# A gated mix of full and windowed attention on one core: a scheduler's constants laid out stretch by stretch, x turned in bf16, and scaled V in one GpSimd operation

## The chip, the cores and the metric

One core of a Trainium2 chip. Times are device microseconds of one execution; the profile's span runs from the first to the last instruction and is about 2 us shorter. Most executions of a kernel agree within 0.3%. A ratio below is the mean time of one kernel's fast runs over that of the other's of the same rounds, so it is not quite the ratio of the medians that stand beside it.

## The reference, cut to what matters

```python
# S = 2048 tokens, D = 640, H = 32 heads of Dh = 20
def A(x, wqkv, wo):                       # full attention
    q, k, v = heads(x @ wqkv)
    p = softmax(q @ k.T * Dh ** -0.5)     # 2048 x 2048 for each of 32 heads
    return merge(p @ v) @ wo
def B(x, wqkv, wo):                       # 8 keys at distances 0, 2, ..., 14 back
    ...
g = sigmoid((x * gate_w).sum(-1))
return g * A(x, ...) + (1 - g) * B(x, ...)
```

The cost is in A's 32 x 2048 x 2048 exponentials: 2048 blocks of 128 keys x 512 queries, one head each.

## The kernel before

It is one Python program that plays a *model* of the engines while it records instructions: every task gets a start and an end in the model, and the next task is chosen by what the model says is free. The order in which the tasks come out is the program, and each engine runs its own list in that order. So a small change of any duration or constant can change the whole order.

A score tile holds two or three blocks. TensorE makes it (`qk`), ScalarE turns it into exponentials (`exp`), and two iterations later TensorE multiplies by V (`pv`). There are two score buffers, so the score matmul of tile s waits for the exponentials of tile s-2. A block can also "ride": it goes into the spare third bank, and the vector engine (DVE) makes its exponential as an integer approximation (`uD`) with three shifted copies (`eD`), each multiplied by V scaled by a constant (`vS`). The more blocks ride, the less ScalarE has to do.

```python
def exp(s):                                            # ScalarE
    T("act", actc(512 * n), lambda e: e.activation(
        ebuf[s % NE][:, 0:512 * n], score[s % 2][:, 0:512 * n], ACTF.Exp, scale=LN2 / STEP), ...)

def gen_d(d):                                          # a quad of up to 4 riding blocks
    ...
    for k in range(1, K):                              # K = 4
        T("pool", 0.7, lambda e, k=k: e.tensor_scalar(
            vS[:, d % 2, k - 1, :], vA_of(kb, q), WEIGHTS[k], None, op0=ALU.mult), ...)   # GpSimd, 84 columns
    for k in range(1, K):
        ...
        T("dve", 0.11 + 0.1334 * n, lambda e, k=k, sl=sl: e.tensor_scalar(
            eD[:, sl % NS, 0:512 * n], uD[d % 2][:, 0:512 * n], SHIFTS[k], None, op0=ALU.add), ...)

def filler(limit):                                     # matmuls on nothing, to keep TensorE active
    if sch.load(2.3) >= FILL:
        return False
    ...

def spend(limit):                                      # side work until the next score matmul is due
    while True:
        run_side(limit)
        ...
        if now + 0.32 > limit or ... or not filler(limit):
            clock[0] = now + 0.2

SLACK = (0.3, 0.68)                                    # how long after exp(s-1) side work may go on
XTOL = 0.17; DTIME = 12.0; BOOST = 4.1; ...            # some 18 constants, the same for the whole run
...
while pvg < NG:
    us = next_tile(); qk(s); exp(s)
    if ...: pv_slot(s)
    spend(exps[s - 1].end + SLACK[len(us) - 2]); s += 1
# the start, once: x in, transposed on TensorE into f32 PSUM, copied to SBUF
turn(0, 0, 3, 0); turn(0, 3, 5, 1)                     # 3 chunks in one score buffer, 2 in the other
x_out: ScalarE copies 3 x 512 columns, DVE 2 x 512
```

## Time and profile before

| | before |
|---|---|
| time, median (lowest to highest) | 863.25 us (862.87 to 863.6) |
| span of the profile | 860.4 us |
| exponentials on ScalarE | 732 for 1736 blocks |
| first exponential starts, last ends | 20.70 us, 848.48 us |
| need at the shortest spacing | 777.6 us |
| loss | 43.5 us |
| tail | 11.9 us |

*Need* and *loss* are worked out from the trace's records. The shortest start-to-start spacing of two exponentials is 904 ns for two blocks and 1331 ns for three, so 427 ns a block and 50 ns an instruction; the need is the sum of that. The loss is what the spacings of all exponentials add up to, less the need, less other ScalarE work between them (6.5 us). Start + need + other + loss + tail is the span.

The page before: busy time by engine, the chain of waits by engine, and three groups (line, engine, operation, tiles, count, then busy us and mean ns of one, then idle time before them).

```profile
span 860.4 us, 30961 instructions
...
PE 837.2 (97%) x13299; PEld 310.4 (36%) x13302; DVE 692.4 (80%) x1178; ACT 820.2 (95%) x766; POOL 220.4 (26%) x333
...
PE 77%; ACT 15%; DVE 4%; issue 3%; POOL 1%; DMA 1%; DVEq 0%; ACTq 0%
...
L1432 ACT ACTIVATE ebuf<-score 128x1024 bf16<-128x1024 f32 (+1 forms) x732 | 804.5, 1197 | 19.9 <-PE score L1409 16.0
...
L720 POOL TENSOR_SCALAR vS<-vA 128x84 bf16<-128x84 bf16 x234 | 140.7, 604 | 230.7 <-PE obank L1477 186.4
L728 DVE TENSOR_SCALAR eD<-uD 128x2048 int16<-128x2048 int16 x234 | 160.2, 709 | 10.3 <-PE obank L1477 9.9
```

ScalarE is 95% busy and TensorE 97%. But the 837 us of TensorE contain 408 quads (four matmuls side by side) of filler, 88 us at 216 ns each, the commonest start-to-start spacing of quads in this trace, and the exponentials' 804.5 us contain waiting: they need 777.6. Of the 43.5 us of loss only 16 us appear as ScalarE waiting for a score matmul.

The waits before (who waited for whom: us, times, longest), three lines:

```profile
ACT ebuf L1432 <- PE score L1409: 16.0, 41, 1.0
...
PEld obank L1477 <- POOL vS L720: 8.8, 33, 0.9
...
PEld obank L1477 <- DVE uD L1422: 1.6, 6, 0.5
```

And the start in two views of the same trace, the timeline of ScalarE and the groups of DVE:

```profile
20.70 1.02 ACT L1432 ACTIVATE ebuf<-score 128x1024 bf16<-128x1024 f32 x1 [0.79 <-PE score L1409]
```

```profile
L1141 DVE CAST xT<-score 128x1024 bf16<-128x1024 f32 x4 | 4.9, 1225 | 3.9 <-PE score L1125 3.9
```

### The profile page before, as it was taken

The numbers are of one execution on the slowest core, as the hardware profiler recorded it, in microseconds if no ns is written. First come the engines' busy times: TensorE is split into PE (matmuls) and PEld (weight loads), VectorE is DVE, ScalarE is ACT, GpSimd is POOL, SyncE is SP. The second block draws the span as 40 slices with busy tenths as digits, with TensorE's granted clock in tenths as the row PEclk, the third lists the DMA queues.
The fourth block names the chain that finished last, engine by engine and source line by source line (L and its number), as shares of the span: only waits on it lengthen the run. The fifth ranks groups of instructions, "written<-read, shape, count | busy, mean of one in ns | idle before, by whom it ended". The sixth has DMA issues, their size and how long they took to land.

```text
span 860.4 us, 30961 instructions
## 1 busy us (share of the span) xinstructions
PE 837.2 (97%) x13299; PEld 310.4 (36%) x13302; DVE 692.4 (80%) x1178; ACT 820.2 (95%) x766; POOL 220.4 (26%) x333
## 2 busy tenths in 40 slices
PE   8999999999999999999999999999999999999997
PEld 4333333343333433333333333333333333333323
DVE  6567787898888889887988879789798878989763
ACT  5999999999999999999999999999999999999994
POOL 5032042721322222221111223222142223123310
PEclk9999999999999999999999999999999999999999
DMA  9112231001010100011010000110010001100000
GB/s 300 33 30 54 45 73 32 16 13 30 25 28 20 38 11 21 5 44 39 18 33 17 6 19 21 32 47 8 20 28 20 6 17 33 46 6 21 14 6 32
DMA packets 40892, 28.16 MB, mean 33 GB/s; under 512 B 23733, under 2 KB 39557, under 8 KB 40757
## 3 DMA queue, kind: packets, MB, share of 16 engines
q1 hardware_dynamic: 40756, 26.20, 11.7%
q8 instruction: 105, 1.72, 0.8%
q14 instruction: 31, 0.25, 0.1%
HBM read 11.94 MB, written 2.62 MB: 17 GB/s over the span
## 4 chain that ended last, share of the span: by engine, by line
PE 77%; ACT 15%; DVE 4%; issue 3%; POOL 1%; DMA 1%; DVEq 0%; ACTq 0%
PE score L1409 23%; PE side L489 19%; PE obank L1477 18%; ACT ebuf L1432 14%; PE score L489 6%; PE obank L1498 4%; PE score L1498 3%; PE side L1498 1%; PE score L615 1%; PE side L814 1%; DMA oTd<-in_A_x_dram 1%; DVE uD L1422 0%; DVE oTt L689 0%; PE score L1125 0%; ACT xT L1139 0%
## 5 line engine op out<-in xcount | busy, mean ns | idle before, releaser
L1432 ACT ACTIVATE ebuf<-score 128x1024 bf16<-128x1024 f32 (+1 forms) x732 | 804.5, 1197 | 19.9 <-PE score L1409 16.0
L1409 PE MATMUL score<-qT,kT 32*128 32x512 bf16 x2048 | 292.1, 384 | 8.7 <-ACT ebuf L1432 6.3
L1422 DVE TENSOR_SCALAR uD<-score 128x512 int16<-128x512 f32 x312 | 208.5, 684 | 41.8 <-PE score L1409 39.3
L720 POOL TENSOR_SCALAR vS<-vA 128x84 bf16<-128x84 bf16 x234 | 140.7, 604 | 230.7 <-PE obank L1477 186.4
L728 DVE TENSOR_SCALAR eD<-uD 128x2048 int16<-128x2048 int16 x234 | 160.2, 709 | 10.3 <-PE obank L1477 9.9
L1409 PEld LDWEIGHTS score<-qT,kT 32*128 32x128 bf16 x2048 | 72.1, 91 | 260.9 <-issue 131.5
L1477 PE MATMUL obank<-ebuf,vA 128*21 128x512 bf16 x1736 | 160.8, 384 | 2.2 <-DVE oTt L689 0.8
L489 PE MATMUL side<-xT,kvw 128*32 128x256 bf16 (+2 forms) x2530 | 102.5, 279 | 0.9 <-DVE dst L593 0.6
L695 POOL TENSOR_TENSOR rcp<-rcp,gA 128x16 f32<-128x16 f32 x31 | 12.3, 397 | 345.3 <-DVE rcp L693 320.8
L1477 PE MATMUL obank<-eD,vS 128*21 128x512 bf16 x936 | 81.0, 379 | 0.0
L489 PEld LDWEIGHTS side<-xT,kvw 128*32 128x32 bf16 (+1 forms) x2530 | 60.5, 96 | 35.0 <-issue 19.8
L1477 PEld LDWEIGHTS obank<-ebuf,vA 128*21 128x21 bf16 x1736 | 39.0, 89 | 81.3 <-issue 63.6
L1498 PE MATMUL obank<-xT,zero 128*32 128x512 bf16 x664 | 56.0, 383 | 0.0
L1498 PE MATMUL score<-xT,ident 128*32 128x512 bf16 x628 | 53.0, 381 | 0.1
L800 DVE TENSOR_TENSOR stage<-qkvB 128x1280 bf16<-128x1280 bf16 x64 | 53.0, 855 | 0.1
L877 DVE TENSOR_TENSOR stage<-qkvB,repB 128x1280 bf16<-128x1280 bf16 x64 | 52.1, 838 | 0.0
L489 PE MATMUL side<-stage,ident 128*32 128x512 bf16 (+1 forms) x768 | 48.7, 346 | 0.0
L784 DVE CAST qkvB<-side 128x512 bf16<-128x512 f32 (+1 forms) x72 | 41.7, 589 | 6.7 <-PE side L489 6.1
L700 POOL TENSOR_TENSOR oN<-oTt,rcp 128x512 bf16<-128x512 f32 x31 | 34.8, 1122 | 2.4
L689 DVE STREAM_TRANSPOSE oTt<-obank 128x512 f32<-128x512 f32 x32 | 22.8, 712 | 14.5 <-PE obank L1477 14.3
L1477 PE MATMUL obank<-uD,vA 128*21 128x512 bf16 x312 | 30.3, 379 | 0.0
L1477 PEld LDWEIGHTS obank<-eD,vS 128*21 128x21 bf16 x936 | 23.4, 92 | 17.5 <-issue 2.5
(167 smaller groups left out, 639.0 us busy)
## 6 DMA issues: line engine op xcount, KB each, us to landing
repB<-eB SPq DMA_DIRECT2D x128, 32.0 KB
WqP<-in_A_wqkv_dram SPq DMA_DIRECT2D x16, 160.0 KB
stage<-in_B_wqkv_dram SPq DMA_DIRECT2D x1, 2400.0 KB
oTd<-oN SPq DMA_DIRECT2D x108, 20.0 KB
qT<-dst SPq DMA_DIRECT2D x104, 20.0 KB
out_dram<-outsb SPq DMA_DIRECT2D x12, 160.0 KB
kvw<-in_A_wqkv_dram SPq DMA_DIRECT2D x2, 800.0 KB
oTd<-in_A_x_dram SPq DMA_DIRECT2D x2, 640.0 KB
```

The source lines that it names most:

```text
L489: ins = e.matmul(o[j:k, :], l[:, j:k], r, start=(first and i == 0), stop=(last and i == n - 1), skip_group_check=True)
L700: T(en, c2, lambda e: e.tensor_tensor(oo, ii, ib, ALU.mult), reads=["rcp", "oTt"], writes=["oN0"])
L720: T("pool", 0.7, lambda e, k=k: e.tensor_scalar(vS[:, d % 2, k - 1, :], _ap(vA, (kb * NQ + q) * 4 * DV, [[1, 4 * DV]]), WEIGHTS[k], None, ...
L728: T("dve", 0.11 + 0.1334 * n, lambda e, k=k, sl=sl: e.tensor_scalar(eD[:, sl % NS, 0:512 * n].bitcast(I16), uD[d % 2][:, 0:512 * n].bitcas ...
L784: t = TB(dvc(n * TOK), lambda e, o=o, i=i: e.tensor_copy(o, i), reads=[("side", b)], writes=[key])
L800: TB(dvc(CN * TOK, 2), lambda e, w=w, ks=ks: e.tensor_tensor(prodB(w), qB[:, :, :], ks, ALU.mult), reads=["qB", "kB"], writes=[("prod", w) ...
L877: TB(dvc(CN * TOK, 2), lambda e, w=w, vs=vs, rr=rr: e.tensor_tensor(prodB(w), vs, rr, ALU.mult), reads=["vB", ("repB", w4 % 2)], writes=[( ...
L1409: ins = e.matmul(o, kT[32 * j:32 * j + 32, q, kb * P:(kb + 1) * P], qT[g % NQT][32 * j:32 * j + 32, :], start=True, stop=True)
L1422: t = T("dve", 0.69, lambda e: e.tensor_scalar(uD[d % 2][:, 512 * i:512 * (i + 1)].bitcast(I16), side[x], UOFF, 0.0, op0=ALU.add, op1=ALU. ...
L1432: exps[s] = T("act", actc(512 * n), lambda e: e.activation(ebuf[s % NE][:, 0:512 * n], score[s % 2][:, 0:512 * n], ACTF.Exp, scale=LN2 / S ...
L1477: ins = e.matmul(obank[32 * j:32 * j + DV, :], v, src, start=(kb == 0), stop=(last and k >= len(lst) - 4), skip_group_check=True)
L1498: ins = e.matmul(o[32 * j:32 * j + 32, :], w[:, 32 * j:32 * j + 32] if best else w[:, :], xT[:, 0, 0:512], start=bool(best), stop=bool(bes ...
```

## The change

The intent: a look-ahead search on the model picks the 18 constants anew for each stretch of ten or more tiles (57 entries); the start is shortened; and GpSimd makes the three scaled V of a quad at once.

```diff
+PLAN = {
+    0: ((0.3, 0.7), 0.26, 2.5, 1.0, 1.0, -1.0, 0.0, 12.0, 7.0, 9.64, 0.4, 0.5, 4.5, 4.21, 0.0, 0.85, 2, 0.0),
+    20: ((0.3, 0.7), 0.12, 2.5, 6.6, 1.0, -1.0, 0.0, 12.0, 7.0, 9.0, 0.5, 0.5, 4.5, 4.0, 0.0, 0.85, 2, 0.0),
 ... 54 entries cut; from tile 320 on most have SLACK (0.23, 0.48) and later FILL 0.77 to 0.8
+    730: ((0.23, 0.48), 0.39, 2.5, 6.6, 0.69, -0.91, 0.1, 9.78, 7.0, 10.56, 0.47, 0.49, 6.24, 1.5, 0.2, 0.89, 1, -3),
+}
@@ main loop
+        plan = PLAN.get(s) if acting else None
+        if plan:
+            (SLACK, XTOL, XPRIO, XLATE, DWAIT, DIDLE, DIDLE2, DTIME, DLOW, DLATE, DVE_AHEAD, DAHEAD, BOOST, XBOOST, RFILL,
+             FILL, HOLD, BOFF) = plan
@@ loads
     x_load(0, 4.2)
-    T("sp", 5.5, ... wk0 ...)
     x_load(1, 5.5)
-    T("sp", 6.0, ... wq0 ...)
-    x_load(2, 7.0)
-    x_load(3, 8.5)
+    T("sp", 6.0, ... wk0 ...)
+    x_load(2, 6.9)
+    x_load(3, 8.2)
+    T("sp", 9.0, ... wq0 ...)
@@ gen_d
-        for k in range(1, K):
-            T("pool", 0.7, lambda e, k=k: e.tensor_scalar(vS[:, d % 2, k - 1, :], ..., WEIGHTS[k], None, op0=ALU.mult), ...)
+        T("pool", 1.0, lambda e: e.tensor_tensor(
+            vS[:, d % 2, :, :], _ap(vA, ..., [[0, K - 1], [1, 4 * DV]]), _ap(vw, 0, [[1, K - 1], [0, 4 * DV]]), ALU.mult), ...)
@@ start: all five chunks of an x tile in one score buffer, as bf16
+                    ins = e.matmul(scb[s_][:, c * 512 + blk * P:...], _ap(xt, ...), ident[:, :],
+                                   start=True, stop=True, is_transpose=True, skip_group_check=True)
-        T("act", actc(1536), ...xT[:, 0:3, cols]...)
-        T("dve", dvc(1024), ...xT[:, 3:5, cols]...)
+        T("act", actc(1024), ...xT[:, 0:2, cols]...)
+        T("dve", dvc(1536, 2), ...xT[:, 2:5, cols]...)
 ... the first Q is projected after the last K, one block of V instead of two is made before the first scores, x_out(3) moves ahead of k_out(1) on ScalarE; a dozen default constants change
```

## The prediction

> **What bounds the kernel now.** ScalarE's stream of exponentials, interlocked with TensorE. The page gives ACT 820.2 us busy of 860.4 (95%), of which the exponentials are 804.5 us in 732 instructions. The chain of waits is PE 77%, ACT 15%, DVE 4%: they hand the score banks back and forth. In the timeline, the shortest start-to-start spacings of exponentials are 904 ns (1024 columns) and 1331 ns (1536): 427 ns per 512 columns plus 50 ns. So 1736 units in 732 instructions need 777.6 us. First start 20.7 us, last end 848.5. The difference, 827.8 - 777.6 - about 7 (other ACT work) leaves roughly 43 us lost, only 16 us of it shown as ACT waiting for PE; the rest hides in "busy" instructions. Tail after the last exponential: 11.9 us. DVE (80%) and GpSimd (26%) are not limits.
>
> **What changes** (instruction orders of both):
>
> 1. Exponentials: 1720 units in 738 instructions, because DVE takes 328 score blocks instead of 312 (82 quads for 78). ACT need: 1720 x 0.427 + 738 x 0.050 = 771.1 us, -6.5 us, all critical. DVE pays 16 x 0.68 + 12 x 0.71 = +19 us, off the path.
> 2. Schedule. TensorE fillers fall from 408 quads to 306 (87 to 65 us at 0.213 us). Summing PE work between successive score matmuls, with durations read from the trace, against the exponential it must fit under: the local excess falls from 100 to 73 us. The measured loss was about 0.43 of that sum, so I estimate -12 us of loss (between -4 and -18). This main term is the most doubtful: stretch by stretch the excess tracked the loss badly.
> 3. Start. wq0 now loads after all of x, wk0 after x1, x is transposed to bf16 PSUM in one score buffer. The DVE copy is 1536 bf16 columns: the Trainium skill ("VectorE: DVE Perf Modes", Why PSUM operands drop a tier) caps a PSUM operand at 2x and f32 at 1x; the f32 copy of 1024 took 1225 ns, so I estimate 0.95 us, and ACT 1.03 instead of 1.45. But Q is now projected last, serially. First exponential near 19 us: -1.8 us.
> 4. Scaled V: 234 GpSimd operations of 604 ns (140.7 us) become 82. From 397 ns at 16 and 1122 ns at 512 two-input columns I estimate 0.75 us each, 61 us. PE weight loads waited 8.8 us for vS (33 times); what part is critical lies within term 2.
> 5. Tail: about 50 small fold matmuls more stand after the last exponential: +0.9 us.
>
> Sum: -6.5 - 12 - 1.8 + 0.9, about -19; shaded to -17, since a plan fitted to a model gains less on the chip.
>
> **Prediction: 846 us, 8 in 10 within 838 to 856. Faster by over 2%: 0.48; within 2%: 0.50; slower: 0.02.**
>
> **What would show it.** ACT exponential busy near 785-790; ACT start-to-start loss near 31 us; first exponential at 18.5 to 19.5 us; the x copy of DVE below 1.1 us; POOL busy near 140 us; DVE near 710; PE fillers 65 us with granted clock still 0.99 or more; tail near 12.8 us.
>
> **What would make it wrong.** The model's instants are off, so that score matmuls still come late (loss stays 40 us: 857); fewer fillers let the TensorE clock drop; DVE, now about 84% busy, delays uD and holds a score bank; the bf16 PSUM copy runs at 1x (1.75 us) and eats the start.

## The result

| | before | after |
|---|---|---|
| time, median (lowest to highest) | 863.3 us (862.87 to 863.6) | 850.52 us (850.09 to 851.37) |
| ratio of fast runs, 95% interval | | 0.9854 (0.9836 to 0.9871) |
| span of the profile | 860.4 | 848.7 |
| exponentials, blocks | 732, 1736 | 738, 1720 |
| first exponential starts | 20.70 | 19.90 |
| need | 777.6 | 771.1 |
| loss | 43.5 | 38.3 |
| tail | 11.9 | 12.9 |
| granted clock | 0.998 | 0.998 |

By term, in us of the span: start -0.8, need -6.5, loss -5.2, tail +1.0, together -11.5 of the measured -11.7.

The page after, the lines that answer to those of before:

```profile
span 848.7 us, 30119 instructions
...
PE 821.5 (97%) x12957; PEld 299.7 (35%) x12957; DVE 716.4 (84%) x1212; ACT 809.6 (95%) x770; POOL 142.0 (17%) x181
...
PE 73%; ACT 14%; DVE 8%; issue 5%; SPq 0%; DMA 0%; DVEq 0%; ACTq 0%
...
L1500 ACT ACTIVATE ebuf<-score 128x1024 bf16<-128x1024 f32 (+1 forms) x738 | 796.5, 1187 | 17.6 <-PE score L1477 14.7
...
L792 DVE TENSOR_SCALAR eD<-uD 128x2048 int16<-128x2048 int16 x246 | 174.1, 734 | 3.0 <-PE obank L1545 2.3
...
L784 POOL TENSOR_TENSOR vS<-vA,vw 128x252 bf16<-128x252 bf16 x82 | 62.9, 769 | 259.7 <-PE obank L1545 259.7
```

The exponentials' busy time fell by 8 us, and their loss only by 5. GpSimd fell by 78 us. Two things were not foreseen: DVE doubled its share of the chain, and one eD takes 734 ns on average where it took 709. The first exponential (timeline):

```profile
19.90 1.45 ACT L1500 ACTIVATE ebuf<-score 128x1536 bf16<-128x1536 f32 x1 [2.10 <-PE score L1477]
```

The waits after: the wait for vS is gone from the list, and TensorE now waits 8.8 us for eD before the V matmuls; no such wait stands in the list of before.

```profile
ACT ebuf L1500 <- PE score L1477: 14.7, 36, 2.1
...
PEld obank L1545 <- DVE eD L792: 5.3, 15, 1.1
...
PE obank L1545 <- DVE eD L792: 3.5, 7, 0.9
```

Where the loss sits can be read from the records tile by tile: take each exponential that started more than 30 ns after the one before it allowed, and ask what TensorE was doing when the score matmul was due. Before, in 193 of 197 such cases TensorE was still in its own earlier work (39.0 us of 39.3); after, in 178 of 181 (33.8 of 34.0). The work just ahead was most often a multiplication of eD by scaled V: 17.5 us of lateness before, 10.5 after. So the loss is TensorE coming late to the score matmul, not ScalarE or the hand-over.

### The profile page after: what moved, and what is told of

Read it like the earlier page. It is cut to its first block, busy times and chain, and to the rows that moved or that the text cites. A ratio compares the mean times of both kernels' runs of the same rounds, so it can differ in the third digit from the quotient of the medians.

```text
span 848.7 us, 30119 instructions
## 1 busy us (share of the span) xinstructions
PE 821.5 (97%) x12957; PEld 299.7 (35%) x12957; DVE 716.4 (84%) x1212; ACT 809.6 (95%) x770; POOL 142.0 (17%) x181
## 4 chain that ended last, share of the span: by engine, by line
PE 73%; ACT 14%; DVE 8%; issue 5%; SPq 0%; DMA 0%; DVEq 0%; ACTq 0%
PE score L1477 22%; PE obank L1545 18%; PE side L554 16%; ACT ebuf L1500 13%; PE score L554 8%; PE obank L1566 4%; DVE eD L792 2%; PE score L1566 2%; DVE uD L1490 1%; PE side L878 1%; DVE stage L864 1%; PE score L1193 1%; PE obank L457 1%; DVE oN L767 1%; PE score L680 0%
## 5 line engine op out<-in xcount | busy, mean ns | idle before, releaser
L1500 ACT ACTIVATE ebuf<-score 128x1024 bf16<-128x1024 f32 (+1 forms) x738 | 796.5, 1187 | 17.6 <-PE score L1477 14.7
L1490 DVE TENSOR_SCALAR uD<-score 128x512 int16<-128x512 f32 x328 | 220.9, 684 | 45.7 <-PE score L1477 42.0
L792 DVE TENSOR_SCALAR eD<-uD 128x2048 int16<-128x2048 int16 x246 | 174.1, 734 | 3.0 <-PE obank L1545 2.3
L784 POOL TENSOR_TENSOR vS<-vA,vw 128x252 bf16<-128x252 bf16 x82 | 62.9, 769 | 259.7 <-PE obank L1545 259.7
L554 PE MATMUL side<-xT,kvw 128*32 128x256 bf16 (+1 forms) x2470 | 101.7, 281 | 0.7 <-DVE qkvB L848 0.6
L1545 PE MATMUL obank<-eD,vS 128*21 128x512 bf16 x984 | 86.0, 379 | 0.0
L760 POOL TENSOR_TENSOR rcp<-rcp,gA 128x16 f32<-128x16 f32 x31 | 12.3, 395 | 386.6 <-DVE rcp L758 367.2
L554 PEld LDWEIGHTS side<-xT,kvw 128*32 128x32 bf16 x2470 | 58.4, 96 | 34.9 <-issue 16.7
L1545 PEld LDWEIGHTS obank<-ebuf,vA 128*21 128x21 bf16 x1720 | 38.6, 89 | 89.3 <-issue 72.9
L1566 PE MATMUL obank<-xT,zero 128*32 128x512 bf16 x688 | 58.5, 383 | 0.0
L1566 PE MATMUL score<-xT,ident 128*32 128x512 bf16 x380 | 33.7, 381 | 0.0
L1545 PEld LDWEIGHTS obank<-eD,vS 128*21 128x21 bf16 x984 | 24.5, 91 | 15.5 <-issue 1.8
```

Source lines behind the costliest of these rows:

```text
L554: ins = e.matmul(o[j:k, :], l[:, j:k], r, start=(first and i == 0), stop=(last and i == n - 1), skip_group_check=True)
L784: T("pool", 1.0, lambda e: e.tensor_tensor(vS[:, d % 2, :, :], _ap(vA, (kb * NQ + q) * 4 * DV, [[0, K - 1], [1, 4 * DV]]), _ap(vw, 0, [[1, ...
L1490: t = T("dve", 0.69, lambda e: e.tensor_scalar(uD[d % 2][:, 512 * i:512 * (i + 1)].bitcast(I16), side[x], UOFF, 0.0, op0=ALU.add, op1=ALU. ...
L1500: exps[s] = T("act", actc(512 * n), lambda e: e.activation(ebuf[s % NE][:, 0:512 * n], score[s % 2][:, 0:512 * n], ACTF.Exp, scale=LN2 / S ...
L1545: ins = e.matmul(obank[32 * j:32 * j + DV, :], v, src, start=(kb == 0), stop=(last and k >= len(lst) - 4), skip_group_check=True)
L1566: ins = e.matmul(o[32 * j:32 * j + 32, :], w[:, 32 * j:32 * j + 32] if best else w[:, :], xT[:, 0, 0:512], start=bool(best), stop=bool(bes ...
```

## The experiments

Two theories stood against each other at first. *Vanished wait*: the loss fell because TensorE no longer waits for the scaled V. *Order*: the wait never mattered, and the plan's order brought the fall. To tell them apart the order of everything else has to stay. That is done by leaving the model's durations as they are and changing only what is emitted: the instruction lists of TensorE, ScalarE and DVE were compared with the kernel's and were equal, unless said otherwise.

All measured values at a glance (start, need, loss and tail in us from each run's profile; the ratio is to the kernel before, from the same rounds). A profile is one execution and not always a middle one: e4_no_fill's is the fastest of its four (850.0 us), e9_thin_swap's the slowest (846.3), and e13_thin65_swap's is at 845.0.

| run | time | ratio (95%) | start | need | loss | tail |
|---|---|---|---|---|---|---|
| before | 863.3 | 1 | 20.70 | 777.6 | 43.5 | 11.9 |
| after | 850.5 | 0.9854 (0.9836 to 0.9871) | 19.90 | 771.1 | 38.3 | 12.9 |
| a0_after, again | 850.25 | 0.9857 (0.9840 to 0.9873) | 19.32 | 771.1 | 38.6 | 12.9 |
| e1_three_vs | 847.63 | 0.9824 (0.9809 to 0.9839) | 19.79 | 771.1 | 35.5 | 12.9 |
| e2_before_one_vs | 863.25 | 1.0005 (0.9990 to 1.0020) | 21.24 | 777.6 | 44.1 | 11.9 |
| e4_no_fill | 852.76 | 0.9882 (0.9857 to 0.9907) | 19.53 | 771.1 | 37.7 | 12.9 |
| e5_old_load_order (one look) | 851.25 | | 20.07 | 771.1 | 38.6 | 12.9 |
| e7_old_constants | 875.05 | 1.0142 (1.0125 to 1.0159) | 19.49 | 779.9 | 47.9 | 19.2 |
| e8_thin | 844.75 | 0.9793 (0.9779 to 0.9808) | 19.43 | 771.1 | 31.3 | 12.9 |
| e9_thin_swap | 843.22 | 0.9781 (0.9764 to 0.9798) | 19.09 | 771.1 | 34.1 | 12.9 |
| e10_one_input | 849.44 | 0.9840 (0.9825 to 0.9855) | 19.42 | 771.1 | 36.6 | 12.9 |
| e11_three_two_input | 848.67 | 0.9831 (0.9816 to 0.9846) | 20.01 | 771.1 | 36.4 | 12.9 |
| e12_plan_shift | 869.86 | 1.0080 (1.0063 to 1.0097) | 19.55 | 783.4 | 42.3 | 15.5 |
| e13_thin65_swap | 843.39 | 0.9779 (0.9766 to 0.9792) | 19.88 | 771.1 | 32.1 | 12.9 |

### The scaled V in three operations again, in the kernel after

```diff
-        T("pool", 1.0, lambda e: e.tensor_tensor(vS[:, d % 2, :, :], ...), ...)
+        def scaled(e):
+            for k in range(1, K):
+                ins = e.tensor_scalar(vS[:, d % 2, k - 1, :], ..., WEIGHTS[k], None, op0=ALU.mult)
+            return ins
+        T("pool", 1.0, scaled, ...)
```

> The kernel after, with the scaled V of a quad made by three GpSimd operations again, inside one task, so that every other instruction stands where it stood. After lost 38 us of the exponentials' stream against their shortest spacing, before 43. Theory A: most of that 5 us is the vanished wait of the weight loads for the scaled V (8.8 us in 33 places before, none after); then the wait comes back to 5 to 9 us and the time goes from 850.5 up to 854 to 858. Rival B: the wait was off the critical path and the 5 us is the plan's order; then the wait comes back but the time stays within 850 to 852.

Measured: 847.63 us, ratio 0.9824 against 0.9854 and 0.9857. Neither range was met: taking this part of the change back makes the kernel 2.8 us *faster* (0.0033 of 863). On the same chip its executions took 847.4 to 848.0 us, those of the kernel after 850.1 to 851.1. Of the two theories it is still *order* that survives: with three operations in the new order the loss is 35.5 us, 8 below before, so the order brings more than the whole fall of 5.2 and the single operation takes part of it back. How much of the 8 us is owed to the 102 filler quads fewer was not tested alone; at the rate of e8_thin below (219 quads, 4.2 us) it would be about 2 us, an estimate. The groups of this run:

```profile
L795 DVE TENSOR_SCALAR eD<-uD 128x2048 int16<-128x2048 int16 x246 | 168.9, 712 | 2.9 <-PE obank L1548 2.3
...
L786 POOL TENSOR_SCALAR vS<-vA 128x84 bf16<-128x84 bf16 x246 | 146.8, 597 | 211.3 <-PE obank L1548 200.8
```

and its waits:

```profile
PEld obank L1548 <- DVE eD L795: 3.9, 11, 1.1
...
PE obank L1548 <- DVE eD L795: 2.1, 4, 0.9
...
PEld obank L1548 <- POOL vS L786: 1.6, 4, 0.7
```

GpSimd is busy 84 us longer, and its wait comes back with only 1.6 us, so the wait had gone mostly because of the order. What the three operations give is a faster eD: 712 ns on average for 734, 5.2 us in all, of the 6.3 us that the durations of all DVE operations fell by. The same two eD of both kernels, in the timelines of DVE and GpSimd. After:

```profile
519.88 1.96 DVE L792 TENSOR_SCALAR eD<-uD 128x2048 int16<-128x2048 int16 x2
...
519.68 1.62 POOL L784 TENSOR_TENSOR vS<-vA,vw 128x252 bf16<-128x252 bf16 x2
```

This run:

```profile
517.40 1.34 DVE L795 TENSOR_SCALAR eD<-uD 128x2048 int16<-128x2048 int16 x2
...
517.23 4.16 POOL L786 TENSOR_SCALAR vS<-vA 128x84 bf16<-128x84 bf16 x5
```

The two eD take 1.96 us beside the two long operations and 1.34 us beside the short ones, which give way instead: five of them last 4.16 us. A third theory follows. *Shared way to SBUF*: a GpSimd operation and an eD that run side by side hold each other up, and the new operation moves the burden from GpSimd, which has time, to DVE, on whose results TensorE waits. The Trainium skill ("GPSIMD Engine Reference", 1. Specifications) says that GpSimd's SBUF interfaces are shared with VectorE and contended by DVE operations in a two-port mode. The trace does not name an eD's mode, but it agrees, and has the size: in the kernel after an eD with no GpSimd operation beside it takes 681 ns (199 cases), one beside a vS operation 997 ns (29 cases).

That mean needs sorting by which began first. An eD that began while a vS was running took 1027 ns (17 cases; in this run 707, 48 cases); one that began before the vS took 689 (7 cases), and then the vS was the long one, 992 ns. In the other five another GpSimd operation was already running. One quad in both kernels, the vS first by 0.05 to 0.06 us. After:

```profile
234.48 1.09 DVE L792 TENSOR_SCALAR eD<-uD 128x2048 int16<-128x2048 int16 x1
...
234.42 0.61 POOL L784 TENSOR_TENSOR vS<-vA,vw 128x252 bf16<-128x252 bf16 x1 [3.29 <-PE obank L1545]
```

This run:

```profile
233.85 0.75 DVE L795 TENSOR_SCALAR eD<-uD 128x2048 int16<-128x2048 int16 x1
...
233.80 0.91 POOL L786 TENSOR_SCALAR vS<-vA 128x84 bf16<-128x84 bf16 x1 [2.07 <-PE obank L1548]
```

The long operation runs through and the eD waits; the first of the short ones waits for the eD (0.91 us, where one with no DVE operation beside it takes 0.42).

### One operation, but in the kernel before

> The kernel before, with one GpSimd operation for the scaled V of a quad, the scheduler's model still charged for three, so that the order is that of before (but for eight small matmuls that stand one tile later). Theory A: the 8.8 us of waits for the scaled V go and the time falls from 863.3 to 855 to 860, loss of the exponentials' stream from 43 to 36 to 39 us. Rival B: the time stays within 861.5 to 863.5.

The edit put the single operation in place of the third of three and let all waits for any of them go to it; three small memsets for the weights were added, with no duration in the model.

Measured: 863.25 us, ratio 1.0005. The *vanished wait* falls a second time. In this order the single operation does not slow eD either (711 ns on average, before 709). The weight loads' waits in this run:

```profile
PEld obank L1480 <- DVE uD L1425: 4.8, 19, 0.5
...
PEld obank L1480 <- DVE eD L731: 2.7, 8, 0.9
```

The wait for vS fell from 8.8 to 0.9 us, but the V matmuls then waited for uD (4.8, before 1.6) and eD (2.7, and 0.8 more on the matmul itself): 9.2 us in all where there were 10.4. The vS operation had been the last of several to arrive, and the next was just behind it.

### Second input, or length?

The single operation differs from the three in two ways: it reads two tensors, and it is one long operation. The first kernel below gives a wrong result on purpose (one weight for all three parts); the comparison with the reference let it pass within its tolerance.

```diff
 one operation, one input (wrong weights):
+        T("pool", 1.0, lambda e: e.tensor_scalar(vS[:, d % 2, :, :], _ap(vA, ..., [[0, K - 1], [1, 4 * DV]]), WEIGHTS[2], None, op0=ALU.mult), ...)
 three operations, two inputs each:
+                ins = e.tensor_tensor(vS[:, d % 2, k - 1, :], ..., _ap(vw, k - 1, [[0, 4 * DV]]), ALU.mult)
```

> The kernel after with the scaled V of a quad in one GpSimd operation over the same 252 columns, but with one input and one weight for all three parts: a wrong result on purpose. Theory A (the second input of the GpSimd operation is what slows the DVE operation beside it): eD beside it falls from 997 ns to 800 or less and the time to 846 to 848.5. Theory B (one long operation, wherever its inputs come from, holds the DVE longer than three short ones): eD beside it stays above 900 ns and the time at 849.5 to 851.

> The kernel after with the scaled V in three GpSimd operations of 84 columns, each with two inputs, as the single one has; a right result. Theory A (second input): eD beside it above 850 ns, time 849.5 or more. Theory B (length of one operation): eD beside it about 770 ns, time 847 to 848.5, as with three one-input operations.

| scaled V | eD beside it, mean (cases) | all eD, sum | loss | ratio |
|---|---|---|---|---|
| one operation, two inputs (after) | 997 ns (29) | 180.5 us | 38.3 | 0.9854 |
| one operation, one input | 882 ns (35) | 178.5 us | 36.6 | 0.9840 |
| three operations, two inputs | 860 ns (39) | 176.4 us | 36.4 | 0.9831 |
| three operations, one input | 772 ns (63) | 175.3 us | 35.5 | 0.9824 |

Neither theory is right alone. Counting only eD that began while a vS was running gives the same order: 1027 ns (17 cases), 844 (23), 773 (31) and 707 (48), together 5.9, 3.7, 2.8 and 1.2 us above 682 ns each. But the first step is not clean: the one-input operation over 252 columns is longer than the two-input one (median 842 ns for 610), so dropping the input changed the length too. Each step lowers the eD time and the loss, and splitting does a little more than dropping the second input. The neighbouring ratios' intervals overlap; the ends of the table (0.9854 and 0.9824) are apart by about as much as one interval is wide, and the order of the four is the same in eD time, loss and ratio. So the sum of both properties costs about 2.8 us; how it divides is only indicated.

### Fillers left out

TensorE lateness is what the loss consists of, and fillers are TensorE work without a result. The kernel after has 306 quads of them, before had 408.

```diff
+    to, kept, owed = {}, [], []
+    for t in sch.lists["pe"]:
+        if t in fillers:
+            to[t] = kept[-1]; owed += t.deps          # waits pass to the next matmul task
+        else:
+            t.deps = list(dict.fromkeys(t.deps + owed)); owed = []; kept.append(t)
```

> The kernel after with all 306 quads of filler matmuls left out of the program but kept in the model, so that everything else stands in the same order. Theory A (fillers sit in real gaps, and the matmul load without them still holds the clock): granted clock 0.99 or more, time within 849 to 852. Rival B (fillers stand before late score matmuls and delay them): 843 to 848. Rival C (fillers hold the clock up): granted clock below 0.98 and time above 856.

Measured: 852.76 us (850.04 to 855.25), granted clock 0.978 to 0.988: in none of the three ranges, with a loss of the clock as in theory C and earlier score matmuls as in B. Busy time by stretch in this run (the stretch and its length in us; busy us of PE, PEld, DVE, ACT and POOL, each with its number of instructions in brackets; then the granted clock, the DMA share and GB/s):

```profile
150.00:170.00 20.00, 18.31 (x251) 6.14 (x248) 17.99 (x29) 18.57 (x18) 9.93 (x11) 0.83 0.07 14
170.00:770.00 600.00, 543.56 (x8698) 200.18 (x8696) 537.97 (x892) 592.38 (x558) 88.11 (x115) 1.00 0.09 23
770.00:802.00 32.00, 26.01 (x240) 6.25 (x243) 26.47 (x40) 28.83 (x28) 4.08 (x6) 0.68 0.08 21
```

The clock was lost in only two stretches (in the 3.4 us ahead of the first loss in each, matmuls covered 57% and 61% of the time, from the records), and exponential by exponential the run gained on the kernel after (the first of its two profiles) in between: 0.1 us behind at tile 150, 3.5 us ahead at tile 690, and 0.2 us ahead again at tile 720, after the second stretch. So fillers do hold the clock, in a few places, and elsewhere they make score matmuls late.

### Fillers only where they hold the clock

The next kernel has the three vS operations and keeps a filler only where other matmul work in the last 3.4 us of the model is under 60%: 87 quads of 306. In its profile 4 of them fall between 140 and 160 us and 22 between 760 and 800, about where the clock was lost, the other 61 thinly elsewhere.

> The kernel after with the scaled V in three operations as in the first experiment (847.6) and with 87 of the 306 filler quads left, those where the other matmul work of the last 3.4 us in the model is under 60%; all else in the same order. Leaving all out cost the clock in three places, which were the places kept here. Theory A (a filler that is not needed for the clock delays the score matmul behind it): clock 0.995 or more and 842.5 to 846. Theory B (fillers fill real gaps): 847 to 848.5. If the clock drops below 0.99: above 848.

> The kernel after, unchanged, on the same chip as the runs beside it: 850 to 851.5, first exponential at 19.4 to 20.0 us, eD operations that run beside a scaled-V operation near 1000 ns.

Measured: 844.75 us, ratio 0.9793, beside the kernel after with 850.25 us on the same chip (as expected; its first exponential, 19.32 us, came just ahead of the 19.4 to 20.0 expected). TensorE's busy time is 40 us below that of the kernel after and the clock is held in the profiled run:

```profile
PE 781.6 (93%) x12081; PEld 282.6 (34%) x12081; DVE 710.4 (84%) x1212; ACT 806.6 (96%) x770; POOL 225.7 (27%) x345
```

Against the three vS operations alone (0.9824) this is 2.7 us more, theory A. The four executions are not equal, though: 844.0, 844.0, 845.5 and 846.7, the last at a clock of 0.996.

### The start

> The kernel after with the loads in the order of before (wk0 after x0, wq0 after x1), the scheduler's model given the same landing times, so that all else stands in the same order. If the new load order is what brings the start forward, the first exponential comes 0.6 us or more later than in after (20.4 or later). If the start's gain is the shorter copies, 0 to 0.3 us later. From the landings of before I expect the second, the third and fourth x landing 0.3 us later.

```diff
     x_load(0, 4.2)
-    x_load(1, 5.5)
-    T("sp", 6.0, ... wk0 ...)
+    T("sp", 6.75, ... wk0 ...)
+    x_load(1, 4.75)
+    T("sp", 10.5, ... wq0 ...)
 ... and so on: each landing stays where the model had it
```

Measured in one look: first exponential at 20.07 us, 0.17 us after that of the kernel after, at the same instant of the full clock (6.2 us in both). That is in the second expected range: the new load order is worth about 0.2 us, by one execution; the rest of the start's gain is in the copies and the order, which were not separated. The chip adds a spread of its own: the kernel after started its exponentials at 19.90 us where the full clock was granted at 6.2 us, and at 19.32 where it was granted at 4.2. Six other runs with this start lie between 19.42 (full clock at 4.4) and 20.01 (6.4). The kernel before had its 20.70 with the full clock at 4.4, so the fairer comparison is with 19.32: about 1.4 us gained.

In the kernel after, the fourth K projection waits for an eviction that stands behind a copy of x on ScalarE (timeline):

```profile
14.22 0.68 ACT L1237 ACTIVATE kT<-obank,onesrow 128x512 bf16<-128x512 f32 x1
...
15.05 1.24 PE L1216 MATMUL obank<-xT,kvw 128*128 128x512 bf16 x5 [0.70 <-ACT kT L1237]
```

> The kernel of the run before with one exchange on ScalarE in the start: the second K eviction ahead of the copy of the fourth x. In after the fourth K projection waited 0.7 us for that eviction, because its bank was held. Expected: first exponential 0.3 to 0.5 us earlier than in the run before, and the time as much less. Rival: the copy of x is later by 0.3 to 0.7 us and holds the projection just as long, no change within 0.15 us.

```diff
+    a = sch.lists["act"]
+    i, j = a.index(swap[0]), a.index(swap[1])      # x_out(3), k_out(1)
+    a[i], a[j] = a[j], a[i]
```

The exchange needs one thing more: who waited for the later of the two must now wait for both, or it reads x before it is there. Measured: first exponential at 19.09 us against 19.43, although the full clock came 0.6 us later in this run. The start is earlier by 0.34 us. The times, 843.22 and 844.75, have overlapping intervals, so they do not show it, and this profiled run, the slowest of the four (846.3 us; the others 843.0 to 843.2), lost the clock once for 3.4 us near the end.

### Is it the plan?

> The kernel after with an empty plan and the scheduler's constants of before: start, load order and scaled V are new, the plan is gone. Its order has 1740 units in 743 exponentials, a need of 779.9 us against 777.6 before and 771.1 after. Theory A (plan is worth its counts, 8 to 9 us, and the scaled V the rest): 857 to 861. Rival B (the plan is worth nearly all of the gain): 861 to 866. Rival C (start and scaled V are worth nearly all): 850 to 855.

```diff
-PLAN = { ... }
+PLAN = {}
-    XTOL = 0.2; SLACK = (0.3, 0.7); ...              # the defaults that the change altered
+    XTOL = 0.17; SLACK = (0.3, 0.68); ...            # as before
```

Measured: 875.05 us. All three theories fall: the new start and the new vS task under the old constants are 12 us *slower* than before. Against the kernel after, the span's 24.5 us are need +8.8, loss +9.6, tail +6.3 and start -0.4. The old constants, which gave 863 us before, are poor ones for the course that the scheduler takes from the new start.

> The kernel after with every entry of the plan taking effect two score tiles later (of 738). If the plan's constants are good settings for their stretch of the work, little changes: 849 to 856. If they are fitted to one course of the scheduler, the course breaks: its order has 1744 units in 779 exponentials, a need of 783.4 us against 771.1, so 12 us more from that alone and a loss of 40 to 48 us: 863 to 875.

```diff
-        plan = PLAN.get(s) if acting else None
+        plan = PLAN.get(s - 2 if s else 0) if acting else None
```

Measured: 869.86 us, in the range of the second expectation. Two tiles of 738 are enough to lose 19 us: need +12.3, loss +4.0, tail +2.6. The plan is no set of good constants for kinds of work; it is the record of a search along one course. One shift was tried; that others break it too is to be expected, not shown.

### A last version

> The kernel of the earlier run with three scaled-V operations, thinned fillers and the exchange on ScalarE (843.2, with one execution of four at 846.3), but keeping a filler where other matmul work of the last 3.4 us is under 65% instead of 60%: 136 of 306 quads. If the slower executions of that run were losses of the clock, they go: all executions within 843 to 844.5 with a granted clock of 0.998 or more. If fillers cost in proportion to their number, the median is 0.5 to 1 us above 843.2.

Measured: 843.39 us (842.62 to 845.73), ratio 0.9779: with e9_thin_swap (843.22) the fastest here, 7 us under the kernel after and 2.2% under before. The expectation failed in the spread: two executions of five were at 845.0 and 845.7 us with clocks of 0.998 and 0.994, and the profiled one has one half-clock spell of 3.4 us, at 659 us, where no earlier run had one. In the 3.4 us ahead of it matmuls covered 57% of the time on the chip; the rule had counted in the model's time. Keeping 49 quads more did not make the clock safe.

## Why the prediction was right or wrong

850.5 us lie within the range of 838 to 856, and 4.5 us above the 846 that were named. "Within 2%", given 0.50, came true. The terms alone came to -19.4 us, 7.7 more than the span lost; that 846 is no further off owes 2 us to the shading, which rested on no reading of the trace. Point by point:

- **What bounds it: right.** The loss hidden in busy exponentials is real, and removing TensorE work without touching ScalarE lowered it (e8_thin: 35.5 to 31.3 against e1_three_vs, from which it differs in the fillers alone).
- **Term 1, exponentials, -6.5 us: right.** 738 instructions for 1720 blocks; the need is a count. But "DVE pays, off the path" was too easy: DVE went from 692 to 716 us, its share of the chain from 4% to 8%, and V matmuls wait for eD.
- **Term 2, schedule, -12 us: mis-sized; it measured -5.2 us (43.5 to 38.3).** This is the step that failed. About 2.8 us of the missing 6.8 are the single vS operation, by e1_three_vs: with three operations in the same order the loss is 35.5. The rest is the factor: the estimate took 0.43 us of loss per us of local excess from the kernel before; with three vS operations the kernel after has 35.5 / 73 = 0.49. What sets that factor was not settled. Within the range given, -4 to -18, the term still lay.
- **Term 3, start, -1.8 us: half right.** The bf16 copy takes 958 ns, as estimated, and ScalarE's 1.02 us. The start gained 0.8 us in the profile beside the result and 1.4 in the second; the two differ in the instant at which the full clock was granted (6.2 and 4.2 us; 4.4 before). A bank held for 0.7 us, which the prediction did not see, cost 0.3 us or more (e9_thin_swap).
- **Term 4, scaled V: the cost right, the effect wrong.** 769 ns and 62.9 us were measured for an estimated 0.75 us and 61. But GpSimd's time was free, and what the operation does to the eD beside it was left out: in this order it costs 2.8 us. That the 8.8 us of waits would be worth something "within term 2" is not borne out: e2_before_one_vs took the waits away in the order of before, and the ratio was 1.0005 (0.9990 to 1.0020).
- **Term 5, tail, +0.9 us: right** (+1.0).
- **Signs:** POOL 142 us and the copy of x were met; the first exponential (19.90) missed its window of 18.5 to 19.5 in one profile and met it in the other; DVE is 716 for 710; ScalarE's exponentials are 796.5 us, not 785 to 790, and the loss 38, not 31, which is the failure of term 2 again.
- **What would make it wrong:** "the model's instants are off, so that score matmuls still come late" is what held. The clock stayed at 0.998 with the fillers that the plan left.

The start's bf16 copy rests on the Trainium skill ("VectorE: DVE Perf Modes", Why PSUM operands drop a tier): 16-bit data from PSUM can go at twice the rate, f32 cannot. The groups of the kernel after agree: 1536 columns in 958 ns, where 1024 in f32 took 1225.

```profile
L1209 DVE COPY xT<-score 128x1536 bf16<-128x1536 bf16 x4 | 3.8, 958 | 3.3 <-PE score L1193 3.3
```

## What to carry to other kernels

Judge an instruction on an idle engine also by what it does to its neighbours: here a GpSimd operation that halved GpSimd's time slowed the DVE operation that started just behind it from 681 to about 1090 ns, and DVE's result was the one awaited. A wait in the profile is worth nothing if the next input arrives just behind it; undo one thing in the same order before believing the number. And constants that a search found for one course of a scheduler are part of that course: after any other edit, search again or freeze the order.

## What the Trainium skill lacked or had wrong

- "GPSIMD Engine Reference", 1. Specifications, names the shared SBUF interfaces, and no page of the skill has durations for such a pair of operations: a DVE `tensor_scalar` over 2048 int16 columns took 681 ns alone, 997 ns beside a two-input GpSimd operation of 252 columns, 772 ns beside one-input operations of 84 (means; who began first decides, as shown above).
- "GPSIMD Engine Reference", 3.1 and 4.1, make two-input elementwise operations the slow ones and one-input ones nearly line-rate (f32). Here, in bf16, it was the other way round: at 252 columns the shortest `tensor_tensor` took 603 ns and the shortest `tensor_scalar` 835, at 84 columns 320 and 409. The second input is a broadcast here and the 252-column forms repeat vA, so this is not the page's own case.
- "TensorE: Matmul & The Clock Gate", What's actually happening, has the clock go by how busy TensorE has been, and names an idle window of about 3.4 us for the half clock. The half-clock spells here agree with the window (3.41, 6.83 and 13.65 us), but TensorE was not idle before or in them: without fillers, the 3.4 us ahead of the three losses of the clock were covered by matmuls to 57, 61 and 65%, with no gap longer than 1.14 us. The page has no busy share at which it happens.
- The same page, Part 4: PE-mode transpose, gives about 275 ns for a 128x128 transpose in a kernel. Here the profile gives each 219 ns at the full clock (ends of matmuls are modelled), and they overlap: twenty in a row took 1.28 us, their starts 56 ns apart, the same as twenty plain matmuls with the identity before (1.29 us). The page has no figure for a row of them.
